# An SSM and sparse-MLP mix on one core: first projection in pairs of chunks with N=512 matmuls, gate in one column-tiled pass, first loads in their order of use

## The chip, the cores and the metric

The kernel runs on one core of a Trainium2 chip. The metric is device time in microseconds of one execution. Most executions of the kernel before agree within 1%. A ratio quoted here is the mean time of one kernel's fast runs over the mean of the other's fast runs of the same rounds, so it is not quite the ratio of the medians that stand beside it. Engine names: PE is TensorE, DVE VectorE, ACT ScalarE, POOL GpSimd, SP the sequencer that issues most DMA loads. L268 is line 268 of the kernel in question, so the same work has different line numbers in different kernels.

## The reference, cut to what matters

```python
# x: [1, 2048, 1024] bf16
g = sigmoid((x * gate_w).sum(-1, keepdims=True))

# a: a diagonal complex state-space layer with 1024 states
Bu = einsum("bld,pd->blp", x, B_bar)            # first projection: "S1" below
for t in range(2048):
    h = Lam_bar * h + Bu[:, t]                  # the scan
a = 2 * einsum("blp,dp->bld", hs, C).real + x * Dskip    # second projection: "S2"

# b: the 8 tokens with the largest r = x @ w_r go through a gated MLP (F = 3584)
y = (silu(x_sel @ w_gate) * (x_sel @ w_up)) @ w_down     # scaled by sigmoid(r), added to x
return g * a + (1 - g) * b
```

## The kernel before

Time is cut into 8 chunks of 256 steps (LC = 256). For each chunk PE does S1 (real and imaginary plane, 8 groups of 128 states), ACT copies the result from PSUM to `V`, and DVE does three multiplies and adds (`dve_m`, a rotation), two scans (`dve_scan`), and three more operations back (`dve_post`), which give `H`. PE's S2 reads `H`. Between these stand the choice of the 8 tokens (`sel_a` to `sel_d`), the expert matmuls (`moe_item`: first gate and up, then, after the SiLU product, down) and the output rows. PE and DVE execute in the order of the program text, as the traces show: in the changed kernel PE stood idle for 3.97 us before the selection matmul (85.40 us), though the S2 matmuls behind it could run (in e3, where they stand before it, they ran in that time), and DVE ran the SiLU products at 207.91 us, behind scan 6, where the text has them. Work is placed by `at((block, place), fn)`.

```python
LC = 256
...
def s1u(k, cp, c, pl):                    # one chunk, N = 256
    ...
    for dc in range(KD):
        nc.tensor.matmul(vps[:, pl, c, :], lhsT=BT[pl][:, dc, ct * P:(ct + 1) * P],
                         rhs=xT[k][:, dc, :], start=(dc == 0), stop=(dc == KD - 1))
...
def gate_cols(k0, k1):                    # r and gate: 8 matmuls with 2 columns per 128 steps
    ...
def sel_b():                              # PE: reads mm, which DVE made in sel_a2
    for k in range(2):
        nc.tensor.matmul(fl_ps[:, k, :], lhsT=ones16[:], rhs=mm[:, k]..., start=True, stop=True)
    ...
def silu_b():                             # DVE: two products; PE's silu_t transposes the result
    ...
gu_pos = [(4, 3)] * 4 + [(4, 6)] * 4 + [(5, 1)] * 4 + ...     # expert weights: single tiles
at((6, 6.1), silu_a); at((6, 6.3), silu_b); at((7, 1.5), silu_t)
d_pos = [(7, 4)] * 7 + [(8, 4)] * 7                            # down items
for n in range(2, NK + 2):
    for cp in range(4):
        if 2 < n < NK and (n, cp) != (3, 0):
            s1(n, cp)                     # S1 of chunk n ...
        run((n, cp + 0.99))
    for i, b in enumerate((2 * (n - 2), 2 * (n - 2) + 1)):
        ...
        s2(b, dh)                         # ... and S2 of chunk n - 2
        run((n, 4 + 2 * i + dh + 0.99))
```

Of the kernel before, what the change touches and what calls it, by code (L numbers as in the profile page):

```python
# [9 lines left out]
ALU = mybir.AluOpType  # L10
# [14 lines left out]
def kernel(  # L25
# [45 lines left out]
    xT = [const.tile([P, KD, LC], BF16, name=f"xT{k}", tag=f"xT{k}") for k in range(5)]  # L71
# [3 lines left out]
    x0r = const.tile([P, BPC, D], BF16, name="x0r", tag="xT5")  # L75
    for tl in range(BPC):
        nc.sync.dma_start(x0r[:, tl, :], x2d[tl * P:(tl + 1) * P, :])
    vrow = small.tile([NCT, 5, P], BF16, name="vrow", tag="va")
    for i, v in enumerate((A_log_dt, A_Lambda_re, A_Lambda_im)):
        nc.scalar.dma_start(vrow[:, i, :], v.rearrange("(c p) -> c p", p=P))  # L80

    def load_xT(k):
        if k >= len(xT):
            xT.append(const.tile([P, KD, LC], BF16, name=f"xT{k}", tag=f"xT{k}"))
        nc.sync.dma_start_transpose(xT[k][:], x2d[k * LC:(k + 1) * LC, :])

    def load_B(c0, c1):
        for pl in range(2):
            nc.sync.dma_start_transpose(BT[pl][:, :, c0 * P:c1 * P], Bsrc[pl][c0 * P:c1 * P, :])  # L89

    load_B(0, 2)
    load_xT(1)
    load_xT(2)
    for c0 in range(2, NCT, 2):
        load_B(c0, c0 + 2)
# [31 lines left out]
    M = {}  # L127
    ones16 = small.tile([NTT, 8], BF16, name="ones16")
# [12 lines left out]
    for tl in range(BPC):  # L141
        xq = ps_s2.tile([P, KD, P], BF16, name="xq", tag="zps")
        for dc in range(KD):
            nc.tensor.transpose(xq[:, dc, :], x0r[:, tl, dc * P:(dc + 1) * P], ident[:])
        (nc.scalar.copy if tl == 0 else nc.vector.tensor_copy)(out=xT[0][:, :, tl * P:(tl + 1) * P], in_=xq[:])
        if tl == 0:
            va_ps = ps_m.tile([P, 3, NCT], BF16, name="va_ps", tag="m")
            for i in range(3):
                nc.tensor.transpose(va_ps[:, i, :], vrow[:, i, :], ident[:NCT, :NCT])
            nc.vector.tensor_copy(vec[:, 0:3, :], va_ps[:])  # L150
# [36 lines left out]
    def tab_arg(q):  # L187
        u = const.tile([P, QC, LC], F32, name="tu", tag="xT7")
# [3 lines left out]
        rn = const.tile([P, QC, LC], F32, name="trn", tag="xT6")  # L192
        nc.vector.tensor_scalar(out=rn[:], in0=u[:], scalar1=MAGIC, scalar2=MAGIC, op0=ALU.add, op1=ALU.subtract)
        f = tabp.tile([P, QC, LC], F32, name="tf", tag="tf", bufs=2)
        nc.vector.tensor_tensor(out=f[:], in0=u[:], in1=rn[:], op=ALU.subtract)
# [17 lines left out]
    def tab_bwd_s(q):  # L213
        f, af = tabs.pop(q)
        S32 = (tabp, const)[q].tile([P, QC, LC], F32, name="tS", tag=("ta", "xT7")[q])
        nc.scalar.activation(out=S32[:], in_=f[:], func=ACT.Sin, scale=TWO_PI)
        C32 = (tabp, const)[q].tile([P, QC, LC], F32, name="tC", tag=("tb", "xT6")[q])
        nc.scalar.activation(out=C32[:], in_=af[:], func=ACT.Sin, scale=-TWO_PI, bias=halfpi[:])
        tabs[q] = (S32, C32)

    def tab_bwd_q(q, c0, c1):
        if c0 == 0:
            S32, C32 = tabs.pop(q)
            q1 = (tabp, const)[q].tile([P, QC, LC], F32, name="tq", tag=("tq", "xT5")[q])
# [22 lines left out]
    def s1u(k, cp, c, pl):  # L247
        if (k, cp) not in vp:
            vp[k, cp] = ps_s1.tile([P, 2, 2, LC], F32, name="vps", tag="vps")
        vps = vp[k, cp]  # L250
        ct = 2 * cp + c
        for dc in range(KD):
            nc.tensor.matmul(vps[:, pl, c, :], lhsT=BT[pl][:, dc, ct * P:(ct + 1) * P], rhs=xT[k][:, dc, :], start=(dc == 0), stop=(dc == KD - 1))  # L253

    def s1e(k, cp):
        if k not in V:
            V[k] = big_new("V", k)
        nc.scalar.copy(out=V[k][:, :, 2 * cp:2 * cp + 2, :], in_=vp.pop((k, cp))[:])  # L258

    def s1(k, cp):  # L260
        for pl in range(2):
            for c in range(2):
                s1u(k, cp, c, pl)
        s1e(k, cp)
# [114 lines left out]
    for pl in range(2):  # L379
        for c in range(2):  # L380
            s1u(0, 0, c, pl)
    s1e(0, 0)
    d0_cp(0, 2)

# [27 lines left out]
    s1(1, 0)  # L412
    d0_cp(2, 4)
    tab_arg(1)
    tab_abs(1)
    tab_bwd_s(0)
    dve_m(0, 0, 2)
    dve_scan0(0, 0, 2)
# [3 lines left out]
    rg = small.tile([P, KD, 2], BF16, name="rg")  # L422
    nc.vector.tensor_copy(rg[:].rearrange("p k t -> p t k"), vb_ps[:])
    gwc = rg[:, :, 1:2]
    tab_bwd_q(0, 0, 2)
    s1(2, 0)
    tab_bwd_q(0, 2, 4)
    tab_bwd_b(0)
    s1(0, 1)
# [4 lines left out]
    s1(1, 1)  # L434
    tab_neg(1)
    d0_cp(4, 8)
    tab_bwd_s(1)
    s1(0, 2)
    tab_bwd_q(1, 0, 2)
    dve_post(0, 0, 4)  # L440
    s1(2, 1)
    tab_bwd_q(1, 2, 4)
    dve_m(0, 4, 6)
    dve_scan0(0, 4, 6)
    s1(0, 3)
# [3 lines left out]
    s1(1, 2)  # L449
    tab_bwd_b(1)  # L450

    def sigm(pool, z_ap, shape, tagp):
        e = pool.tile(shape, BF16, name=tagp + "_e")
# [7 lines left out]
    def gate_cols(k0, k1):  # L461
        n = (k1 - k0) * BPC
        zc = ps_m.tile([P, n, 2], F32, name="zc", tag="m")
        for k in range(k0, k1):
            for tl in range(BPC):
                j = (k - k0) * BPC + tl
                for dc in range(KD):
                    nc.tensor.matmul(zc[:, j, :], lhsT=xT[k][:, dc, tl * P:(tl + 1) * P], rhs=rg[:, dc, :], start=(dc == 0), stop=(dc == KD - 1))  # L468
        sl = slice(k0 * BPC, k1 * BPC)
        zb = small.tile([P, n], BF16, name=f"zb{k0}")  # L470
        nc.scalar.copy(out=zb[:], in_=zc[:, :, 1])
        nc.scalar.copy(out=rcb[:, sl], in_=zc[:, :, 0])
        ex = sigm(small, zb[:], [P, n], f"gc{k0}")

        def rest():
            gb = ex
            nc.vector.tensor_copy(gcol[:, sl], gb[:])
            ob = small.tile([P, n], BF16, name=f"ob{k0}")
            nc.vector.tensor_scalar(out=ob[:], in0=gb[:], scalar1=-1.0, scalar2=1.0, op0=ALU.mult, op1=ALU.add)
            nc.vector.tensor_copy(omgcol[:, sl], ob[:])  # L480
        return rest
# [4 lines left out]
    M["aT"] = small.tile([P, NFC // 4, 4, 32], BF16, name="aT", tag="va")  # L486
    nc.gpsimd.memset(M["aT"][:], 0.0)
    g0 = gate_cols(0, 3)
    s1(1, 3)
    g0()  # L490
    dve_post(0, 4, 8)
# [108 lines left out]
    NW = NGU + NFP  # L600
    wq = {}
# [3 lines left out]
    def load_w():  # L605
        while nload[0] < NW and free_w:
            i = nload[0]
            pool, tag = free_w.pop(0)
            if i < NGU:
                h, r = divmod(i, 2 * KD)  # L610
                dc, k = divmod(r, 2)
                w = pool.tile([P, NG, FH], BF16, name="wgu", tag=tag)
                nc.sync.dma_start(w[:], (wg_v, wu_v)[k][:, dc, h])
            else:
                jp, c = divmod(i - NGU, NFB)
                w = pool.tile([P, 2, D], BF16, name="wd", tag=tag)
                p0 = 0
                while p0 < P:
                    h, o = divmod(c * P + p0, FH)
                    n = min(P - p0, FH - o)  # L620
                    nc.sync.dma_start(w[p0:p0 + n], wd_v[o:o + n, h, 2 * jp:2 * jp + 2, :])
                    p0 += n
            wq[i] = (w, pool, tag)
            nload[0] += 1

    def moe_item(i):
        w, pool, tag = wq.pop(i)
# [20 lines left out]
        free_w.append((pool, tag))  # L648
        load_w()
# [49 lines left out]
    def scatter_upd():  # L699
        nc.gpsimd.indirect_dma_start(out=out2d[:, :], out_offset=bass.IndirectOffsetOnAxis(ap=M["idx_c"][:, :1], axis=0), in_=M["upd"][:], in_offset=None, bounds_check=L - 1, oob_is_err=False, compute_op=ALU.add)  # L700
        pool, tag = free_w.pop(0)
        M["ul"] = pool.tile([P, BPC, D], BF16, name="ul", tag=tag)
# [59 lines left out]
    load_xT(3)  # L762
    load_xT(4)
    for b in range(4):
        load_x(b)
    for k in range(5, NK):
        load_xT(k)
    s1(2, 2)
    s1(2, 3)
    s1(3, 0)  # L770
    dve_m(1, 0, 8)
    dve_scan(1, 0, 8)

    gq = {}
    at((2, 6), lambda: gq.update(r=gate_cols(3, 8)))
    at((2, 7), sel_a)
    at((2, 7.1), lambda: (dve_post(1, 0, 8), gq.pop("r")(), sel_a2()))
    at((3, 4), sel_b)
    at((3, 4.1), sel_b2)
    at((4, 2), sel_c)  # L780
    at((4, 3), sel_d)
    at((4, 5.4), lambda: (sel_c2(), sel_d2()))
    at((3, 4), load_w)
    gu_pos = [(4, 3)] * 4 + [(4, 6)] * 4 + [(5, 1)] * 4 + [(5, 4)] * 4 + [(5, 7)] * 5 + [(6, 2)] * 5 + [(6, 5)] * 6
    for i in range(NGU):
        at(gu_pos[i], lambda i=i: moe_item(i))
    at((6, 6.1), silu_a)
    at((6, 6.3), silu_b)
    at((7, 1.5), silu_t)
    d_pos = [(7, 4)] * 7 + [(8, 4)] * 7  # L790
    for i in range(NFP):
        at(d_pos[i], lambda i=i: moe_item(NGU + i))
    at((8, 4.15), fin_a)
    at((8, 4.17), lambda: (fin_b(), scatter_upd()))

    for k in range(2, NK):
        late = k == 2
        if k == NK - 1:
            at((k, 4.5), lambda: last_m(0))
        else:  # L800
            at((3, 1.3) if late else (k, 4.5), lambda k=k: dve_m(k, 0, 8))
        at((3, 4.2) if late else (4, 0.6) if k == 3 else (k, 4.6), lambda k=k: rows(k - 1))
# [81 lines left out]
```

## Time and profile before

| | before |
|---|---|
| time, median of 4 | 252.34 us (252.07 to 253.46) |
| span of the profiled run | 250.8 us |
| PE / DVE busy | 97% / 93% |
| mean granted TensorE clock | 0.999 |

From the page of the kernel before: span, busy microseconds by engine, granted TensorE clock in 40 equal slices (tenths of full speed), and the chain that ended last, by engine.

```profile
span 250.8 us, 4677 instructions
...
PE 244.3 (97%) x1986; PEld 164.2 (65%) x1986; DVE 232.9 (93%) x230; ACT 101.6 (41%) x143; POOL 41.3 (16%) x58
...
PEclk9999999999999999999999999999999999999999
...
PE 49%; DVE 41%; SPq 3%; DMA 3%; issue 2%; ACT 0%; DVEq 0%
```

Two engines are close to full and share the chain of waits almost evenly. So what one of them gains counts only as far as the other lets it.

Next the costliest matmul groups of the kernel before (line, engine, operation, tiles, shapes, count; busy us and mean ns of one; idle time before them).

```profile
L253 PE MATMUL vps<-xT,BT 128*128 128x256 bf16 x1024 | 114.2, 273 | 1.6 <-DMA BT<-in_A_B_re_dram 0.8
...
L716 PE MATMUL zps<-CT,H 128*128 128x512 bf16 x480 | 105.8, 379 | 0.0
```

The mean of one (273 ns) is a latency; matmuls overlap (1024 times 273 ns would be 280 us, and PE is busy with them for 114.2). The busy time over the count gives the pace: 111.5 ns for N=256, 220 ns for N=512, the changes from one group of work to the next included.

And the places on DVE's timeline (first fence) and on PE's (second) (start, us, engine, line, what; in brackets the idle time just before and what ended it): the start of chunk 1 on DVE, the selection matmul, the SiLU transposes, the down items, the last S2 group.

```profile
52.01 2.29 DVE L277 TENSOR_TENSOR U<-V,T2tab 128x4096 bf16<-128x4096 bf16 x1
```

```profile
85.33 0.27 PE L524 MATMUL fl_ps<-mm,ones 16*8 16x128 bf16 x2
...
194.92 0.56 PE L662 MATMUL aT_ps<-ident,gr 128*128 128x128 bf16 x7 [0.35 <-DVE gr L657]
...
221.42 1.71 PE L647 MATMUL y<-wd,aT 128*32 128x256 bf16 x56
...
240.34 7.11 PE L730 MATMUL zl<-CT,H 128*128 128x512 bf16 x48
```

From 15.6 us to the end PE's longest gap is that 0.35 us. The SiLU transposes come right behind their producer and wait only these 0.35 us for it.

### The profile page before, as it was taken

What the parts mean: (1) busy time and instruction counts of PE and PEld (TensorE: products, weight loads), DVE (VectorE), ACT (ScalarE), POOL (GpSimd) and SP (SyncE); (2) the same over time, 40 slices, a digit from 0 to 9 for tenths busy, and PEclk for the clock granted to TensorE, in tenths of its full rate; (3) what the DMA queues carried; (4) which work ended last, traced back from release to release, by engine and by line L of the source; (5) the groups of instructions that cost most, each with busy time, mean ns of one, the idle gap of its engine ahead of it and who ended that gap; (6) DMA issues with size and microseconds to landing.
All of it is one profiled execution on the core that took longest, in us unless ns stands there. A gap on an engine that the chain in (4) does not pass through costs nothing.

```text
span 250.8 us, 4677 instructions
## 1 busy us (share of the span) xinstructions
PE 244.3 (97%) x1986; PEld 164.2 (65%) x1986; DVE 232.9 (93%) x230; ACT 101.6 (41%) x143; POOL 41.3 (16%) x58
## 2 busy tenths in 40 slices
PE   8799999999999999999999999999999999999994
PEld 5688889884678447874487644876448864454453
DVE  1899999999999599999999999999999999999992
ACT  3679981535212322535121372131732335264411
POOL 4020000000000067201400240013101400141520
PEclk9999999999999999999999999999999999999999
DMA  7999999999900202819795587869999829966072
GB/s 182 228 158 238 179 258 211 251 260 261 312 0 3 73 0 89 167 31 348 156 358 190 203 232 236 277 216 338 262 288 293 183 46 277 302 169 178 3 167 84
DMA packets 63492, 48.31 MB, mean 193 GB/s; under 512 B 49504, under 2 KB 51168, under 8 KB 63472
## 3 DMA queue, kind: packets, MB, share of 16 engines
q1 hardware_dynamic: 59056, 37.23, 56.6%
q0 software_dynamic: 4224, 10.53, 17.5%
q8 instruction: 15, 0.25, 0.4%
q10 hardware_dynamic: 192, 0.27, 0.3%
q14 instruction: 5, 0.04, 0.1%
HBM read 27.55 MB, written 8.40 MB: 143 GB/s over the span
## 4 chain that ended last, share of the span: by engine, by line
PE 49%; DVE 41%; SPq 3%; DMA 3%; issue 2%; ACT 0%; DVEq 0%
PE vps L253 22%; PE zps L716 21%; DVE U L288 14%; DVE U L277 4%; DVE U L279 4%; DVE V L278 4%; DVE U L313 4%; DVE H L315 4%; DVE H L311 4%; DVE xt L691 3%; PE zl L730 3%; DMA xT<-in_A_x_dram 3%; SPq L89 2%; PE y L647 1%; PE zc L468 1%
## 5 line engine op out<-in xcount | busy, mean ns | idle before, releaser
L253 PE MATMUL vps<-xT,BT 128*128 128x256 bf16 x1024 | 114.2, 273 | 1.6 <-DMA BT<-in_A_B_re_dram 0.8
L253 PEld LDWEIGHTS <-BT 128*128 128x128 bf16 x1024 | 99.4, 98 | 15.6 <-issue 1.8
L716 PE MATMUL zps<-CT,H 128*128 128x512 bf16 x480 | 105.8, 379 | 0.0
L716 PEld LDWEIGHTS <-H 128*128 128x128 bf16 x480 | 46.3, 98 | 55.7 <-issue 1.9
L288 DVE TENSOR_TENSOR_SCAN U<-d,U 128x2048 bf16<-128x2048 f32 (+1 forms) x20 | 61.7, 3128 | 0.4
L258 ACT CAST V<-vps 128x1024 bf16<-128x1024 f32 x32 | 32.3, 1009 | 60.9 <-PE vps L253 60.9
L719 ACT ACTIVATE ot<-zps,gcol 128x512 bf16<-128x512 f32 x30 | 20.6, 688 | 67.8 <-PE zps L716 65.0
L693 POOL DMA_DIRECT2D out_dram<-xt x14 | 7.8, 561 | 93.1 <-DVE xt L691 92.6
L687 ACT ACTIVATE e<-Dbc,omgcol,gcol 128x1024 f32<-128x1024 bf16 x16 | 18.9, 1233 | 0.0
L691 DVE TENSOR_TENSOR xt<-xt,e 128x1024 bf16<-128x1024 bf16 x16 | 18.8, 1218 | 0.0
L278 DVE TENSOR_TENSOR V<-V,nTi 128x4096 bf16<-128x4096 bf16 (+1 forms) x10 | 16.5, 1652 | 0.5
L277 DVE TENSOR_TENSOR U<-V,T2tab 128x4096 bf16<-128x4096 bf16 (+1 forms) x10 | 16.5, 1645 | 0.5
L279 DVE TENSOR_TENSOR U<-U,V 128x4096 bf16<-128x4096 bf16 (+1 forms) x10 | 16.5, 1652 | 0.3
L554 POOL DMA_INDIRECT xsel<-in_A_x_dram,idx_c x1 | 6.4, 6387 | 61.3 <-ACT ot L719 61.3
L313 DVE TENSOR_TENSOR U<-U,S2tab 128x4096 bf16<-128x4096 bf16 (+1 forms) x8 | 16.2, 2025 | 0.3
L315 DVE TENSOR_TENSOR H<-H,U 128x4096 bf16<-128x4096 bf16 (+1 forms) x8 | 16.2, 2025 | 0.3
L311 DVE TENSOR_TENSOR H<-U,Ctab 128x4096 bf16<-128x4096 bf16 (+1 forms) x8 | 16.1, 2018 | 0.0
L740 POOL DMA_DIRECT2D out_dram<-ot x14 | 14.3, 1048 | 2.0 <-DMA out_dram<-yc,idx_c 2.0
L682 POOL DMA_DIRECT2D xt<-in_A_x_dram x12 | 8.2, 684 | 13.6 <-DMA out_dram<-xt 13.6
L346 DVE TENSOR_TENSOR_SCAN U<-D,U 128x1024 bf16<-128x1024 f32 x4 | 8.9, 2278 | 0.0
L635 PE MATMUL pgu<-wgu,xsel 128*32 128x448 bf16 x128 | 7.4, 355 | 0.0
L730 PE MATMUL zl<-CT,H 128*128 128x256 bf16 (+1 forms) x48 | 7.1, 308 | 0.0
(145 smaller groups left out, 127.9 us busy)
## 6 DMA issues: line engine op xcount, KB each, us to landing
wgu<-in_B_w_gate_dram SPq DMA_DIRECT2D x16, 448.0 KB, 6.4
wgu<-in_B_w_up_dram SPq DMA_DIRECT2D x16, 448.0 KB, 5.7
wd<-in_B_w_down_dram SPq DMA_DIRECT2D x12, 512.0 KB, 6.7
out_dram<-xt POOLq DMA_DIRECT2D x14, 256.0 KB, 2.8
out_dram<-ot POOLq DMA_DIRECT2D x14, 256.0 KB, 5.9
xt<-in_A_x_dram POOLq DMA_DIRECT2D x12, 256.0 KB, 5.1
xt<-in_A_x_dram SPq DMA_DIRECT2D x4, 256.0 KB, 4.1
wd<-in_B_w_down_dram SPq DMA_DIRECT2D x4, 256.0 KB, 7.8
```

The lines of the kernel that those rows point to most:

```text
L253: nc.tensor.matmul(vps[:, pl, c, :], lhsT=BT[pl][:, dc, ct * P:(ct + 1) * P], rhs=xT[k][:, dc, :], start=(dc == 0), stop=(dc == KD - 1))
L258: nc.scalar.copy(out=V[k][:, :, 2 * cp:2 * cp + 2, :], in_=vp.pop((k, cp))[:])
L277: nc.vector.tensor_tensor(out=u, in0=v, in1=T2tab[:, :, c0:c1, :], op=ALU.mult)
L278: nc.vector.tensor_tensor(out=v, in0=v, in1=bc(nTi, c0, c1), op=ALU.mult)
L279: nc.vector.tensor_tensor(out=u, in0=u, in1=V[k][:, ::-1, c0:c1, :], op=ALU.add)
L288: nc.vector.tensor_tensor_scan(out=fl, data0=d0[:, c0:c1, :].rearrange("p c t -> p (c t)"), data1=fl, initial=0.0, op0=ALU.mult, op1=ALU.add)
L311: nc.vector.tensor_tensor(out=h, in0=g, in1=bc(Ctab, c0, c1), op=ALU.mult)
L313: nc.vector.tensor_tensor(out=g, in0=g, in1=S2tab[:, :, c0:c1, :], op=ALU.mult)
L315: nc.vector.tensor_tensor(out=h, in0=h, in1=G[k][:, ::-1, c0:c1, :], op=ALU.add)
L691: nc.vector.tensor_tensor(out=xt[:], in0=xt[:], in1=es.pop(b)[:], op=ALU.mult)
L716: nc.tensor.matmul(zps[:], lhsT=H[k][:, pl, ct, tl * P:(tl + 1) * P], rhs=CT[pl][:, ct, dsl], start=(ct == 0 and pl == 0), stop=(ct == NCT ...
L719: nc.scalar.activation(out=ots[b][:, dsl], in_=zps[:], func=ACT.Copy, scale=gcol[:, b:b + 1])
```

## The change

The intent: S1 with N=512 (two chunks in one matmul) halves the number of S1 matmuls and weight loads, the gate shrinks from 128 matmuls to 32 on four column tiles, and PE starts earlier because B's first tiles and x1 come in the order of their use. As chunks now come in pairs, the whole order of work was laid out anew: blocks of an S1 pair, two S2 chunks, an S1 pair, and so on. Expert weights are loaded in slots twice as large.

```diff
+    load_B(0, 0, 1)                       # 128 rows of B, real plane
...
+    new_X(0)
+    load_xT(1)
+    load_B(1, 0, 1)
+    for pl in range(2):
+        load_B(pl, 1, 2)
...
-    load_B(0, 2)
-    load_xT(1)
-    load_xT(2)
...
+    def s1u(m, ct, pl, k0, k1):
+        o = vp[m, ct][:, pl, k0:k1, :].rearrange("p k t -> p (k t)")
         for dc in range(KD):
-            nc.tensor.matmul(vps[:, pl, c, :], lhsT=BT[pl][...], rhs=xT[k][:, dc, :], ...)
+            nc.tensor.matmul(o, lhsT=BT[pl][...], rhs=X[m][:, dc, k0 * LC:k1 * LC], ...)
...
+    def gate_rows():
+        for dc in range(KD):
+            for m in range(4):
+                nc.tensor.matmul(zr[32 * m:32 * m + 32, :], lhsT=rg[:, dc, :], rhs=X[m][:, dc, :], ...)
...
+    at((1, 0.5), lambda: dve_post(1, 0, 8))
+    at((1, 1.5), lambda: dve_m(2, 0, 8))
+    at((1, 1.6), sel_a2)                                  # DVE, behind multiply 2
+    at((1, 3.9), sel_b)                                   # PE, needs sel_a2
+    at((2, 1.5), lambda: dve_scan(2, 0, 8))
+    at((2, 2.0), sel_b2)
...
+    at((7, 0.5), lambda: dve_m(6, 0, 8))
+    at((7, 1.5), lambda: dve_scan(6, 0, 8))
+    at((7, 1.95), silu_a)                                 # ACT
+    at((7, 1.96), silu_b)                                 # DVE, behind scan 6
+    at((7, 3.9), silu_t)                                  # PE, needs silu_b
...
+    at((8, 3.92), fin_a)
+    at((8, 3.94), lambda: (fin_b(), scatter_upd()))
+    at((9, 0.0), lambda: last_m(1))
...
+    pos = [(3, 2.9)] * 2 + [(4, 1.9)] * 3 + [(5, 1.9)] * 3 + [(6, 1.9)] * 3 + [(6, 5.9)] * 3 + [(7, 1.9)] * 2 + [(8, 0.9)] * 4 + [(8, 3.9)] * 3
...
+    blocks = [(1, None), (None, 0), (None, 1), (2, None), (None, 2), (None, 3), (3, None)] + [(None, k) for k in range(4, NK)]
```

In `blocks`, (m, None) is the S1 of pair m and (None, k) the S2 of chunk k; S1 pair 0 is in the prologue.

## The prediction

> **What bounds the kernel now.** TensorE and VectorE bound it together. Busy table: PE 244.3 us (97%), DVE 232.9 (93%) of a 250.8 us span; the chain of waits is 49% PE, 41% DVE. By the timeline PE has no gap over 0.4 us from 15.6 us to the end, and DVE waits only 2.45 us (for the selection's `fl`) between 12 and 245 us. So a gain counts only if both engines get it, and neither may be made to wait for the other.
>
> **Removed.** S1 spends 110 ns a matmul at N=256 (96 in 10.6 us), S2 216.5 ns at N=512; halving S1's count saves about 3 ns on each of 512: 1.5 us. [...] The gate goes from 3.2 us (128 matmuls, chain) to 32 column-tiled ones: estimated from the expert matmuls (16 of N=448 in 0.88 us) about 2.2 us with the transposes. First S1 matmul at 6.4 instead of 7.2 us. DVE loses the gate's small operations (0.5 us), the split of post 0 (0.5) and the 2.45 us wait. PE alone would end 2 us earlier.
>
> **Added.** Chunk 0's V now comes at half the rate, two chunks together. Its last quarter comes with the end of S1 pair 0, estimated at 36.9 us (35 without waits for B). DVE, 35.7 us along, waits 0 to 2.4 us, so chunk 1's first multiply starts at about 52.7 us (52.0 before). ACT's evacuations become 64 halves of some 0.6 us; it has room.
>
> **The order, which decides.** S1 pairs alternate with pairs of S2, and engines run in program order. From the trace: multiplies 7.1 us, scans 9.1, post 6.9, S2 chunk 13.85, S1 pair 27.7, a pair of expert items 0.44. The critical path I expect:
> - DVE: multiply 1, scan 1, post 1, multiply 2, first selection part: 31.4 us, to 84.1. PE gets to the next selection matmul (which reads this) at about 81 and waits some 3 us.
> - PE: S2 chunk 1, S1 pair 2, S2 2 and 3, S1 pair 3, 14 pairs of expert items, last evacuation: 104.3 us, to 188.4. DVE, 102.3 us of work, waits about 2 us at multiply 6.
> - DVE: multiply 6, scan 6, SiLU products: 17.5 us, to 205.9. PE stands at the SiLU transposes from about 202.4, a wait of 3.5 us: these products now come behind a whole scan.
> - PE: transposes, S2 5, down items, S2 6 and 7: 45.4 us, to 251.3; before 247.5.
>
> With the same 3.3 us tail the span is 254.6, time about 256.
>
> **Prediction.** 255.8 us, range 252.0 to 259.0; faster by over 2% 0.03, within 2% 0.75, slower by over 2% 0.22.
>
> **What would show it.** Groups: S1 512 matmuls, about 111 us busy in all; gate about 2 us. Waits and timeline: PE waiting for the selection's DVE operations near 81 us and for the SiLU products near 203 us, 2 to 5 us each; DVE waiting for ACT's V cast near 187 us; DVE's multiply 1 starting at 51 to 53.5 us. If PE shows no such gaps, the path is wrong and the time should fall to 250 or lower.
>
> **What would make it wrong.** B or x landing much earlier or later (x6/x7 are wanted by the gate at 61 us and estimated to land then); expert weights late, since a load is twice as large and goes to only two to four buffers (slower); an order of DVE's work that I misread (faster, 249 to 251).

A remark in brackets is cut. No term of the sum goes with it: the 1.5 us saved in S1 rest on the two measured paces that stand there, 110 and 216.5 ns, and the forecast stays 254.6 us for the span and about 256 for the time. ACT's half evacuations, put there at some 0.6 us, took 0.588 us each in the changed kernel (64 of them; 1.009 us for each of the 32 whole ones before).

## The result, and the profile after

| | before | changed |
|---|---|---|
| time, median of 4 | 252.34 us | 267.04 us (264.02 to 269.18) |
| ratio of the fast runs | | 1.0534 (1.0438 to 1.0629) |
| span of the profiled run | 250.8 us | 264.8 us |
| PE / DVE busy | 97% / 93% | 93% / 88% |
| mean granted TensorE clock | 0.999 | 0.974 (0.966 to 0.981 in the four runs) |

The change made the kernel 5.3% slower. The three fast runs lie between 264.02 and 267.38 us (1.3%; those of the kernel before spread over 0.6% here). The fourth, 269.18 us, was marked slow because it is over 1.5% above the fastest; it is in the median and not in the ratio. The same parts of the page for the changed kernel:

```profile
span 264.8 us, 3475 instructions
...
PE 246.8 (93%) x1368; PEld 114.9 (43%) x1392; DVE 232.5 (88%) x221; ACT 104.6 (40%) x176; POOL 36.0 (14%) x60
...
PEclk9999999999999899999999999999999679979999
...
PE 61%; DVE 24%; DMA 7%; SPq 6%; issue 1%; ACT 0%; DVEq 0%
```

Both engines have about as many busy microseconds as before, in a span that is 14 us longer. So neither has more work; they wait, or work more slowly. And the clock, flat before, has three dips.

The matmul group of S1, and the gate on the timeline, show that the intended part of the change worked as meant:

```profile
L268 PE MATMUL vps<-X,BT 128*128 128x512 bf16 (+1 forms) x507 | 111.4, 376 | 2.5 <-DMA BT<-in_A_B_im_dram 1.7
```

```profile
61.66 1.91 PE L483 MATMUL zr<-X,rg 128*32 128x512 bf16 x32
...
66.97 0.39 PE L490 MATMUL zt<-ident,zrb 128*128 128x128 bf16 x4
```

S1 is busy for 111.4 us (13 of its 520 matmul records are missing in this trace; where all 520 are there and no dip falls into S1, in e1, e2 and e10 below, it is 112.6 to 112.8), against 114.2. The gate takes 1.9 us and a fraction for the transposes, against 3.2.

The places on the timelines of the changed kernel that answer to those shown of before, DVE first (the start of chunk 1 and of multiply 6), then PE:

```profile
53.74 2.29 DVE L294 TENSOR_TENSOR U<-V,T2tab 128x4096 bf16<-128x4096 bf16 x1
...
191.49 2.29 DVE L294 TENSOR_TENSOR U<-V,T2tab 128x4096 bf16<-128x4096 bf16 x1 [3.07 <-ACT V L275]
```

```profile
85.40 0.37 PE L538 MATMUL fl_ps<-mm,ones 16*8 16x128 bf16 x2 [3.97 <-DVE mm L530]
...
209.24 0.93 PE L681 MATMUL aT_ps<-ident,gr 128*128 128x128 bf16 x7 [3.62 <-DVE gr L676]
209.96 5.94 PE L734 MATMUL zps<-CT,H 128*128 128x512 bf16 x16
...
230.72 0.40 PE L668 MATMUL y<-wd,aT 128*32 128x256 bf16 x8 [1.50 <-DMA wd<-in_B_w_down_dram]
232.00 0.62 PE L668 MATMUL y<-wd,aT 128*32 128x256 bf16 x8 [0.87 <-DMA wd<-in_B_w_down_dram]
...
254.54 7.11 PE L748 MATMUL zl<-CT,H 128*128 128x512 bf16 x47
```

After the first 20 us PE waits three times: 4.0 us for DVE's first selection part, 3.6 us for the SiLU products, 2.4 us for down weights. In between DVE waits 3.1 us for V. (DVE's longest wait, 7.1 us up to 234.19 for the result of the down items, held up no matmul: the last S2 group starts at 254.54, 3.7 us after its `H` is done at 250.85.) And after a wait PE works slowly: the 16 matmuls at 209.96 take 5.9 us, where 16 of the same shape take 3.6 elsewhere. The table by stretches of time shows why. Columns: stretch; its length and busy us (and instructions) of PE, PE's weight loads, DVE, ACT, POOL; granted TensorE clock; DMA share; GB/s. The rows come in pairs, a wait and what follows it.

```profile
81.40:85.40 4.00, 0.03 (x2) 0.03 (x1) 3.86 (x10) 0.69 (x1) 0.00 (x0) 0.94 0.00 0
85.40:90.20 4.80, 4.79 (x16) 1.90 (x18) 4.80 (x3) 0.36 (x1) 0.00 (x0) 0.69 0.00 0
205.60:209.20 3.60, 0.02 (x1) 0.00 (x0) 3.50 (x6) 0.69 (x1) 0.87 (x1) 0.81 0.74 172
209.20:215.90 6.70, 6.66 (x27) 2.86 (x31) 6.63 (x3) 0.34 (x1) 0.00 (x0) 0.59 0.17 31
228.20:232.60 4.40, 2.02 (x50) 1.21 (x50) 0.00 (x0) 0.69 (x1) 0.00 (x0) 0.90 0.66 197
232.60:240.00 7.40, 7.18 (x31) 3.12 (x30) 5.67 (x7) 2.14 (x5) 3.05 (x2) 0.83 0.07 7
```

Each wait is followed by some microseconds at a clock of 0.59 to 0.83. The lost share of the clock times the length of the stretch is 0.31 x 4.8 + 0.41 x 6.7 + 0.17 x 7.4 = 5.5 us. This is the page's PEclk row seen closely. Asked for the stretches between, the trace gives a clock of 0.50 from 84.96 to 88.37 us, from 207.84 to 214.66 and from 231.73 to 235.14, and 1.00 between these three. So the dips last 3.41, 6.82 and 3.41 us, and each begins 0.3 to 1.4 us before its wait ends.

### The profile page after: what moved, and what is told of

It reads as the page before. It is cut to its first block, busy times and chain, and to the rows that moved or that the text cites. A ratio compares the mean times of both kernels' runs of the same rounds, so it can differ in the third digit from the quotient of the medians.

```text
span 264.8 us, 3475 instructions
## 1 busy us (share of the span) xinstructions
PE 246.8 (93%) x1368; PEld 114.9 (43%) x1392; DVE 232.5 (88%) x221; ACT 104.6 (40%) x176; POOL 36.0 (14%) x60
## 4 chain that ended last, share of the span: by engine, by line
PE 61%; DVE 24%; DMA 7%; SPq 6%; issue 1%; ACT 0%; DVEq 0%
PE vps L268 28%; PE zps L734 27%; DVE U L305 7%; DMA wd<-in_B_w_down_dram 4%; DVE U L294 3%; DVE U L296 3%; DVE V L295 3%; SPq L80 3%; PE zl L748 3%; DMA BT<-in_A_B_im_dram 2%; PE pgu L656 2%; DVE H L332 2%; DVE U L330 2%; DVE H L328 2%; SPq L637 2%
## 5 line engine op out<-in xcount | busy, mean ns | idle before, releaser
L268 PE MATMUL vps<-X,BT 128*128 128x512 bf16 (+1 forms) x507 | 111.4, 376 | 2.5 <-DMA BT<-in_A_B_im_dram 1.7
L734 PE MATMUL zps<-CT,H 128*128 128x512 bf16 x470 | 109.5, 391 | 0.8 <-issue 0.4
L268 PEld LDWEIGHTS <-BT 128*128 128x128 bf16 x520 | 50.1, 98 | 62.2 <-DMA BT<-in_A_B_im_dram 2.6
L734 PEld LDWEIGHTS <-H 128*128 128x128 bf16 x480 | 47.6, 101 | 60.2 <-issue 8.3
L275 ACT CAST V<-vps 128x512 bf16<-128x512 f32 x64 | 34.3, 588 | 54.9 <-PE vps L268 52.5
L330 DVE TENSOR_TENSOR U<-U,S2tab 128x4096 bf16<-128x4096 bf16 x7 | 16.0, 2292 | 0.2
L332 DVE TENSOR_TENSOR H<-H,U 128x4096 bf16<-128x4096 bf16 x7 | 16.0, 2292 | 0.2
L328 DVE TENSOR_TENSOR H<-U,Ctab 128x4096 bf16<-128x4096 bf16 x7 | 16.0, 2280 | 0.0
```

Source lines behind the costliest of these rows:

```text
L268: nc.tensor.matmul(o, lhsT=BT[pl][:, dc, ct * P:(ct + 1) * P], rhs=X[m][:, dc, k0 * LC:k1 * LC], start=(dc == 0), stop=(dc == KD - 1))
L275: nc.scalar.copy(out=V[k][:, :, ct, :], in_=vp[m, ct][:, :, kk, :])
L328: nc.vector.tensor_tensor(out=h, in0=g, in1=bc(Ctab, c0, c1), op=ALU.mult)
L330: nc.vector.tensor_tensor(out=g, in0=g, in1=S2tab[:, :, c0:c1, :], op=ALU.mult)
L332: nc.vector.tensor_tensor(out=h, in0=h, in1=G[k][:, ::-1, c0:c1, :], op=ALU.add)
L734: nc.tensor.matmul(zps[:], lhsT=H[k][:, pl, ct, tl * P:(tl + 1) * P], rhs=CT[pl][:, ct, dsl], start=(ct == 0 and pl == 0), stop=(ct == NCT ...
```

## The experiments

Ten kernels were run. All gave correct results. Up to the gate the changed kernel and e1 to e7 are the same program, and still the gate starts between 60.07 and 61.93 us in their profiled runs, because PE's waits for the first loads vary. So a difference of up to 1.9 us between the spans of two single profiled runs says nothing by itself. The theory at the start, WAITS+CLOCK: the time is lost in PE's three waits, which come from the new order of work, and in the clock dips that they set off; S1 and the gate are as good as they should be. Rivals: that DVE bounds what follows, so waits and dips cost nothing; or that pairs of chunks are themselves slower, by the later start of DVE or by S1.

| run | what it changes | time, median | ratio to before, 95% interval |
|---|---|---|---|
| changed kernel | | 267.04 | 1.0534 (1.0438 to 1.0629) |
| e1_fill | dummy matmuls in two waits | 265.93 | 1.0538 (1.0506 to 1.0570) |
| e2_silu_first | SiLU products before scan 6 | 255.42 | 1.0124 (1.0094 to 1.0153) |
| e3_select_later | selection matmul later | 262.50 | 1.0403 (1.0365 to 1.0440) |
| e4_three_waits | both, and last down items later | 254.03 | 1.0037 (0.9995 to 1.0079) |
| e5_down_later | last down items later, alone | 261.88 | 1.0343 (1.0292 to 1.0394) |
| e6_down_fill | e5 with dummy matmuls | 258.31 | 1.0229 (1.0169 to 1.0289) |
| e7_no_new_waits | e4 without its new wait | 250.40 | 0.9894 (0.9858 to 0.9930) |
| e8_n256 | e7 with S1 at N=256 | 252.94 | 1.0003 (0.9963 to 1.0044) |
| e9_old_loads | e7 with the old first loads | 255.21 | 1.0050 (0.9999 to 1.0101) |
| e10_e7_again | e7 repeated | 250.82 | 0.9894 (0.9833 to 0.9954) |

Besides the one run of the changed kernel, one of e4 (255.94 us) and two of the kernel before beside e9 and e10 (256.34 and 256.23) were slow.

### e1_fill: keep PE at work in the waits, take no wait away

```diff
+    def pefill(n):                       # result never read
+        fz = ps_s2.tile([P, 512], F32, name="fz", tag="zps")
+        for _ in range(n):
+            nc.tensor.matmul(fz[:], lhsT=CT[0][:, 0, 0:P], rhs=CT[0][:, 0, 0:512], start=True, stop=True)
     def sel_b():
+        pefill(8)
...
     def silu_t():
+        pefill(8)
```

> The changed kernel with 8 dummy N=512 matmuls (1.73 us, result unused) in front of the selection matmul and again in front of the SiLU transposes. No wait is taken away: PE is only kept at work in the first half of it. Theory CLOCK (each wait of 3.6 to 4.0 us makes the granted TensorE clock fall to 0.6 to 0.7 for the next 5 to 7 us, which costs 1.5 us after the selection and 2.7 us after the SiLU): both idle stretches shrink to about 2 us, the clock stays at 1.0 after both, and the time falls by about 4 us against the changed kernel (266 to 262). Rival WAITS ALONE (the time is lost in the waits, the clock dip costs nothing because VectorE bounds what follows): within 1 us of 266.

The time did not move: 265.93 us. Read alone, this speaks for the rival. PE's timeline and two rows by stretches of this run show that it does not:

```profile
83.81 0.32 PE L544 MATMUL fl_ps<-mm,ones 16*8 16x128 bf16 x2 [2.23 <-DVE mm L530]
...
207.99 0.56 PE L688 MATMUL aT_ps<-ident,gr 128*128 128x128 bf16 x7 [1.90 <-DVE gr L682]
...
225.90 0.40 PE L674 MATMUL y<-wd,aT 128*32 128x256 bf16 x8 [0.79 <-DMA wd<-in_B_w_down_dram]
228.33 0.62 PE L674 MATMUL y<-wd,aT 128*32 128x256 bf16 x8 [2.03 <-DMA wd<-in_B_w_down_dram]
230.98 0.62 PE L674 MATMUL y<-wd,aT 128*32 128x256 bf16 x8 [2.03 <-DMA wd<-in_B_w_down_dram]
```

```profile
83.80:88.60 4.80, 4.79 (x16) 1.81 (x17) 4.80 (x3) 0.36 (x1) 0.00 (x0) 0.64 0.00 0
...
208.00:214.00 6.00, 6.00 (x88) 3.60 (x89) 5.93 (x3) 1.97 (x3) 0.00 (x0) 1.00 0.20 28
```

Half of the prediction failed: with 2.2 us of idle left at the selection the dip there came all the same (0.64). With 1.9 us left at the SiLU it did not come (1.00), and from the selection matmul to the first down item at 211.94 us this run needed 128.1 us, against 130.4 (215.84 in the changed kernel). What was won was then lost: PE came to the last down items earlier, their weights did not, and the waits for them grew from 2.4 to 4.9 us, with a clock of 0.50 from 228.0 to 231.5 us and 0.77 from there to 238.0 (3.2 us of clock lost), where the changed kernel had 0.90 from 228.2 to 232.6 and 0.83 to 240.0 (1.7 us lost). From the first down item to the start of the last DVE operation it took 48.9 us (211.94 to 260.82), against 45.9 in the changed kernel (215.84 to 261.69). The gain was given back at the weights. e5 and e6 below repeat the test without them.

### e2_silu_first: SiLU products before scan 6

```diff
-    at((7, 1.5), lambda: dve_scan(6, 0, 8))
+    at((7, 1.97), lambda: dve_scan(6, 0, 8))
```

> The changed kernel with the SiLU products put before scan 6 on VectorE instead of behind it, nothing else. Theory WAITS+CLOCK: PE's wait of 3.6 us before the SiLU transposes goes to zero and with it the dip to 0.59 after it; the down items are reached 6 us earlier, but their last three weight pairs then arrive only after PE (load issued when the first pairs are used, 11 us to land), so PE waits there for some 4 us instead of 2.4: time about 4 to 5 us below the changed kernel, near 261.5. Rival VECTOR (VectorE's own work bounds the end, so PE's wait is harmless): within 1 us of 266, or slower by the 1.3 us that VectorE now idles for the sigmoid.

255.42 us: one line of the schedule gives back about 10 of the 13.5 us (1.0534 to 1.0124), twice what was expected. Of the 10.4 us between the two profiled runs, 1.5 had been won before the selection matmul (83.91 against 85.40), by a shorter wait for B. PE's timeline in e2, at the SiLU transposes and at the last down items:

```profile
204.62 0.55 PE L681 MATMUL aT_ps<-ident,gr 128*128 128x128 bf16 x7
...
223.07 0.40 PE L668 MATMUL y<-wd,aT 128*32 128x256 bf16 x8 [0.92 <-DMA wd<-in_B_w_down_dram]
```

PE's wait before the SiLU transposes is gone and no dip follows (a clock of 1.00 from 198 to 214 us); DVE idles 1.55 us for the sigmoid, as expected. The expectation was wrong about the weights: PE waited 0.9 us for them, not 4, and no dip followed (the page's PEclk row has a 9 in every slice from 89 us to the end). From the first down item to the end of the last wait for weights it took 14.5 us (208.55 to 223.07), against 16.2 us in the changed kernel (215.84 to 232.00). One difference is that POOL's row stores, which also go by DMA, began 1.6 us after the first down item in the changed kernel (217.5) and 9.6 us after it here (218.2). That the stores slowed the loads is an inference from these times; no run tests it.

### e3_select_later: the selection matmul two S2 groups later

```diff
-    at((1, 3.9), sel_b)
+    at((2, 1.2), sel_b)
```

> The changed kernel with the selection matmul two S2 groups later on PE (its consumer on VectorE stays where it is, behind scan 2). Theory CHAIN: PE's 4.0 us wait and the dip to 0.69 behind it go, S1 pair 3 ends some 5 us earlier, VectorE no longer waits 3.1 us for V before multiply 6, and the end moves by about that 3 us, not by 5, because PE then waits longer (6 us or more) before the SiLU transposes: about 263. Rival PE BOUND: the whole 5.4 us come back, about 260.5. Rival HARMLESS: no change.

262.50 us, as theory CHAIN had it (263). Two details differ. The gain came through a new wait: PE now reaches the transposes of the selected rows 2.5 us before the gather of these rows has landed, with a dip of its own (a 7 in the page's PEclk row from 97.4 to 103.8 us), so DVE still waits 2.7 us for V. And the wait before the SiLU transposes stayed at 3.6 us, where 6 had been expected.

### e4_three_waits: both moves, and the last down items one S2 block later

```diff
-    at((1, 3.9), sel_b)
+    at((2, 1.2), sel_b)
...
-    at((7, 1.5), lambda: dve_scan(6, 0, 8))
+    at((7, 1.97), lambda: dve_scan(6, 0, 8))
...
-    pos = [...] + [(8, 0.9)] * 4 + [(8, 3.9)] * 3
+    pos = [...] + [(8, 0.9)] * 4 + [(9, 0.9)] * 3
...
+    at((9, 0.92), fin_a)                                   # from (8, 3.92)
+    at((9, 0.94), lambda: (fin_b(), scatter_upd()))        # from (8, 3.94)
+    at((9, 0.95), lambda: last_m(1))                       # from (9, 0.0); last_post, last_scan follow
```

> The changed kernel with both moves and with the last three down-weight pairs, and what depends on them, in the next S2 block (so that their loads have 14 us more). Theory WAITS+CLOCK: no PE wait over 1 us after 20 us, clock 1.0 throughout, and PE's work alone gives an end at about 246 us, span 249, time 250 to 251: 15 us below the changed kernel and 1 to 2 us below the kernel before. The runs should agree within 0.5 per cent, unlike those of the changed kernel (264.0 to 269.2). Rival N=512/ORDER (the pairs of chunks are themselves slower, by the later start of VectorE or by S1 itself): it stays at 256 or above, where the blind schedule without clock or weight waits had put it.

254.03 us, short of the expected 250 to 251, and the runs did not agree within 0.5% as expected: the fast ones lie between 251.81 and 254.28. The three waits are gone; one remains, the new one that e3 had shown: 2.56 us for the gather, with a dip behind it (a clock of 0.82 from 100.6 to 110.0 us, so some 1.7 us lost). Two of the four runs had no such dip (clock 0.999 and 1.0), and still one of them took 254.28 us: not all of the spread comes from the clock. The wait for the gather is what e7 removes.

### e5_down_later and e6_down_fill: the clock alone

e5 takes from e4 only the part about the down items. e6 adds to it the `pefill` of e1, with 14 and 12 dummy matmuls.

> The changed kernel with only the last three down-weight pairs and what depends on them one S2 block later; the waits for the selection and the SiLU stay. Theory LATE WEIGHTS: PE's waits of 1.5 and 0.9 us in the down items, the drain around them (3.7 us from 228.2 to 232.6 in the trace, 0.65 of it work) and the dip behind them go: about 5 us less than the changed kernel, 261. Rival: the down loads are only an effect of the earlier waits and the 5 us return elsewhere: 264 to 267.

> The same as e5_down_later with dummy matmuls in front of the two waits that are left, 14 of N=512 (3.0 us) before the selection matmul and 12 (2.6 us) before the SiLU transposes, so that PE idles about 1 us at each. The first try of this (8 dummies) cleared the dip after the SiLU and not the one after the selection (2.2 us idle left), and gave its gain back in longer waits for the down weights, which are out of the way here. Theory CLOCK: both dips gone, granted clock 0.995 or more, 3.5 to 4 us below e5_down_later, about 257, with nothing but useless work added. Rival WAITS ALONE: equal to e5_down_later within 1 us.

e5: 261.88 us, as expected (261). PE's timeline of e5, the matmuls behind the SiLU transposes and the last down items, which no longer wait:

```profile
210.35 4.62 PE L734 MATMUL zps<-CT,H 128*128 128x512 bf16 x16
...
230.68 1.49 PE L668 MATMUL y<-wd,aT 128*32 128x256 bf16 x48
```

e6: 258.31 us, 1.1% less (1.0229 against 1.0343, each beside the same runs of before), that is about 2.9 us. PE's timeline of e6, and its rows by stretches:

```profile
84.03 0.32 PE L544 MATMUL fl_ps<-mm,ones 16*8 16x128 bf16 x2 [0.94 <-DVE mm L530]
...
206.99 0.56 PE L688 MATMUL aT_ps<-ident,gr 128*128 128x128 bf16 x7 [1.04 <-DVE gr L682]
```

```profile
84.00:89.00 5.00, 4.92 (x23) 2.28 (x25) 5.00 (x3) 1.05 (x2) 0.00 (x0) 1.00 0.00 0
...
207.00:214.00 7.00, 6.89 (x91) 4.08 (x94) 6.93 (x4) 1.97 (x3) 0.00 (x0) 1.00 0.28 56
```

26 matmuls were added whose results nobody reads, nothing else differs, and the kernel became faster: three of the four runs of e6 are below every run of e5. The granted clock was 1.0 in all four runs of e6 and 0.980 to 0.987 in those of e5. And the S2 group behind the SiLU transposes, 4.62 us in e5, takes 3.62 in e6 (207.39 us). So the dips cost time by themselves. The size is below the 3.5 to 4 us expected, and it is uncertain: the two intervals come within 0.0003 of each other. In the profiled run of e5 the dip at the SiLU lost 1.7 us of clock (0.72 from 208.0 to 214.0 us), in that of the changed kernel 3.4 (0.81 from 205.6 to 209.2 us, 0.59 from there to 215.9); and of the 2.9 us between the spans of the two profiled runs, 1.4 us had been won before the selection matmul already (84.03 against 85.45), which the dummies cannot have done, while a new wait for a down weight took 0.6 us back. What is shown is the sign and the place; the size is some 1.5 to 3 us for the two dips of e5.

### e7_no_new_waits

e4 with one more line:

```diff
-    at((3, 0.9), sel_c)
+    at((3, 1.9), sel_c)
```

> e4_three_waits had one new wait: 2.6 us before the transposes of the selected rows, whose gather had not landed, and a dip of 1.7 us behind it. Here these transposes come one S1 group (3.5 us) later. Theory WAITS+CLOCK: no PE wait over 0.7 us after 10 us, clock 1.0, VectorE's 2.8 us wait for V before multiply 6 nearly gone; 3 us below e4_three_waits: about 250.5, some 0.7 per cent faster than the kernel before, and repeatable. Rival: a floor of VectorE's keeps it at 252.5 to 254.

250.40 us, ratio 0.9894, and again 0.9894 in e10 (0.986 to 0.993 expected). The page of e7:

```profile
span 250.1 us, 3474 instructions
...
PE 240.4 (96%) x1367; PEld 113.0 (45%) x1392; DVE 232.1 (93%) x221; ACT 104.4 (42%) x176; POOL 36.1 (14%) x60
...
PEclk9999999999999999999999999999999999999999
```

The clock is flat again and both engines are as full as before. DVE no longer waits for V before multiply 6. The expected limit of 0.7 us for PE's waits after 10 us was missed twice: 1.5 us for B at 18.66 us, and 0.9 us for ACT at 152.78, the longest after 20 us. From the SiLU transposes to the start of the last DVE operation it needs 45.6 us (201.36 to 246.93), against 52.4 in the changed kernel (209.24 to 261.69).

### e8_n256: only the matmul size undone

```diff
     def s1(m, ct):
         for pl in range(2):
-            s1u(m, ct, pl, 0, 2)
+            for kk in range(2):
+                s1u(m, ct, pl, kk, kk + 1)
```

> e7_no_new_waits with S1 in two matmuls of N=256 per weight tile instead of one of N=512, in the same order and the same PSUM tiles; only the matmul size is undone. Theory: S1 loses 3 ns on each of some 500 pairs, 1.5 us of PE work, all on the path if PE bounds the kernel: about 1.5 us above e7_no_new_waits, 252. Rival VECTOR BOUND: no difference within 0.5 us. Rival N=512 IS SLOWER in this order: faster than e7.

252.94 us, ratio 1.0003: N=512 is worth 1.1%, about 2.7 us by the two ratios, where 1.5 was expected. Every run of e8 is slower than every run of e7, so the sign is shown; for the size the two intervals allow anything from under 1 to over 4 us. The traces give PE's part of it. The same stretch of S1 and what follows it, up to the next expert items, first of e7 (80 matmuls of N=512, two records missing), then of e8 (160 of N=256):

```profile
107.55 17.44 PE L268 MATMUL vps<-X,BT 128*128 128x512 bf16 x78
124.83 7.07 PE L734 MATMUL zps<-CT,H 128*128 128x512 bf16 x32
131.83 1.32 PE L656 MATMUL pgu<-wgu,xsel 128*32 128x448 bf16 x24
```

```profile
109.16 17.64 PE L268 MATMUL vps<-X,BT 128*128 128x256 bf16 x160
126.85 6.85 PE L735 MATMUL zps<-CT,H 128*128 128x512 bf16 x31
133.64 1.32 PE L657 MATMUL pgu<-wgu,xsel 128*32 128x448 bf16 x24
```

(124.83 - 107.55) / 80 = 216.0 ns for N=512. (For N=256, 224 matmuls of S1 took 24.46 us in the kernel before, 15.59 to 40.05, so 109.2 ns each.) In e8 the start of the S2 group can't be used in the same way: of its 32 matmuls 31 are recorded, and the missing one is the first, as the time to the expert items is 0.21 us shorter than in e7. From the start of S1 to the expert items it is 24.28 us in e7 and 24.48 in e8. The difference over 80 pairs is 2.5 ns a pair, times 512 is 1.3 us. That is close to the 1.5 us expected, and so is S1's busy time (112.6 to 112.8 us where all records are there, 114.2 in the kernel before). What else makes up the 2.7 us, if it is that much, is open. The first part of the change does what it was meant to do.

### e9_old_loads: only the first loads undone

```diff
-    load_B(0, 0, 1)
...
     new_X(0)
-    load_xT(1)
-    load_B(1, 0, 1)
     for pl in range(2):
-        load_B(pl, 1, 2)
+        load_B(pl, 0, 2)
+    load_xT(1)
```

> e7_no_new_waits with the load part of the change undone: B's first two tiles in 256 rows per plane, both before x1, as in the kernel before. Theory START: x1 lands about 11.5 us instead of 8.2, PE waits some 3 us for it, gets to B's third tile about 1 us later, chunk 0's last quarter comes 1 us later to VectorE, and the whole run moves by about that 1 us: 0.4 per cent above e7. Rival NO MATTER (the DMA queue's total, not the order, sets when S1 pair 0 ends): within 0.3 us of e7.

255.21 us, 1.6% above e10 on the same chip, where 0.4% was expected. The wait for x1 was as foreseen:

```profile
11.84 7.57 PE L266 MATMUL vps<-X,BT 128*128 128x256 bf16 x32 [2.93 <-DMA X<-in_A_x_dram]
```

It brought a dip that the expectation had left out: a clock of 0.66 from 11.8 to 16.0 us, and a mean of 0.991 to 0.993 in all six runs, against 0.998 to 1.0 in e10. The gate began 2.8 us later than in e10 (64.47 against 61.66), and the weights of the down items were once more late, by 1.3 us. So the order of the first loads, the other part of the change, is worth about 4 us in this order of work.

## Why the prediction was right or wrong

The prediction was 255.8 us, range 252.0 to 259.0. The time was 267.0 us: right in its direction, outside its range. Taking the predicted path step by step against the profiled run:

| step, as predicted | predicted | measured | difference |
|---|---|---|---|
| DVE to the first selection part | ends at 84.1 us | 85.4 | +1.3 |
| PE to the last evacuation of S1 pair 3 | 104.3 us | 106.1 (85.40 to 191.49) | +1.8 |
| DVE: multiply 6, scan 6, SiLU products | 17.5 us | 17.75 (to 209.24) | +0.3 |
| PE: transposes to the last matmul | 45.4 us | 52.4 (to 261.69) | +7.0 |

**Right: the path itself.** The order of releases was as predicted, with the three waits at their places: PE for the selection near 81 us (3 us predicted, 4.0 measured), DVE for V near 187 us (2 and 3.1), PE for the SiLU products near 203 us (3.5 and 3.6).

**Right: the parts of the change.** S1's busy time (111 us predicted, 112.6 to 112.8 where all records are there) and the gate (about 2 us) came out. DVE's chunk 1 began at 53.74 us, just beyond the predicted 51 to 53.5. The value of N=512 came out too, in PE's work: 1.5 us predicted, 1.3 by the traces of e7 and e8.

**Wrong: "PE: transposes, S2 5, down items, S2 6 and 7: 45.4 us".** This is the step that failed, as the term that was mis-sized: 52.4 us. Without waits and dips it is right: in e7 the same work took 45.6 us. Two things filled the 7 us. First the clock: the sum had PE's work at full speed right behind each wait. By the lost shares of the clock above, the dips after the SiLU and after the down items cost 2.7 and 1.3 us in this step, and the one after the selection another 1.5 us in the second step. e6 shows that such dips cost time: there PE is held up just as long, only busy with useless work. Second the weights: the last down items took 4.4 us (228.2 to 232.6) where all six of this kind take 1.4 us in e7, so 3.0 us went there. e5 shows it: 4.8 us (1.0534 to 1.0343), for this wait and the dip behind it together, came back when these weights were used one block later. Their late arrival stood in the prediction as a risk, not in its sum.

**Why the clock was missing.** The trace of the kernel before could not show it: after 15.6 us PE's longest wait there is 0.35 us, and the clock is 1.00 up to 250.26 us. The prediction named two waits of 3 and 3.5 us and did not ask what PE would do behind them. That is part of why the range was too narrow upwards: a wait that brings a dip has a second price, here 1.5 and 2.7 us.

**Where the expected gain went.** It is there, and the new order of work covers it. Taken from e7, N=512 brings 1.3 us of PE's work and about 2.7 us of time (e8), and the order of the first loads about 4 us (e9; the dip and the late weights that the old order brings are in this). These do not add up: e7 as a whole is 2.7 us faster than the kernel before. The schedule around them, which put two PE steps behind long operations of DVE and needed 3 MB of weights within three S2 groups (10.4 us), cost more. With the placements of e7 the changed kernel runs at 250.40 us, 1.1% faster than the kernel before.

**Open.** Whether e7's waits of 1.5 us for B in the prologue could go was not tried. That POOL's stores slowed the weight loads is only inferred.

**Which idle stretches were followed by a dip.** No run was made for this; the traces give these cases:

| run | PE idle, up to | clock behind it |
|---|---|---|
| changed kernel | 4.0 us, to 85.40 | 0.69 from 85.4 to 90.2 us |
| changed kernel | 3.6 us, to 209.24 | 0.59 from 209.2 to 215.9 us |
| changed kernel | 1.5 and 0.9 us, to 230.72 and 232.00 | 0.83 from 232.6 to 240.0 us |
| e1 | 2.2 us, to 83.81 | 0.64 from 83.8 to 88.6 us |
| e4 | 2.6 us, to 100.52 | 0.82 from 100.6 to 110.0 us |
| e9 | 2.9 us, to 11.84 | 0.66 from 11.8 to 16.0 us |
| e1 | 1.9 us, to 207.99 | 1.00 from 208.0 to 214.0 us |
| changed kernel | 1.75 us, to 18.39 | 1.00 from 10.0 to 37.6 us |
| e3 | 1.4 and 0.9 us, to 226.88 and 228.20 | 9 in every slice of the PEclk row from 214.2 us on |

In the changed kernel PE was busy for 0%, 35% and 38% of the 3.4 us before the clock fell (at 84.96, 207.84 and 231.73 us). In the 3.4 us from 16.69 us it was busy for 50%, and the clock stayed at 1.00. The two pairs of short waits for weights, 1.5 and 0.9 us in the changed kernel and 1.4 and 0.9 us in e3, are close to each other, and only the first was followed by a dip. So the length of a wait alone does not tell, and what else decides is not shown.

## What to carry to other kernels

Where two engines are both over 90% busy, lay a new order of work out on paper with measured durations, look for every place where an in-order engine meets a producer that sits behind a long operation of another engine, and move the short producer in front of the long operation: here one line, the SiLU products before a scan, was worth some 9 to 10 us. Price a PE wait at the wait plus the clock lost behind it: here the single waits of 2.2 to 4.0 us in the table above were followed by stretches that lost 1.4 us (0.34 x 4.2, e9) to 2.7 us (0.41 x 6.7, changed kernel). And when removing a wait gains nothing, look for the next resource that was just in time, here a weight load, before concluding that the wait was harmless.
